# Expert feed-forward with 216 token slots an expert and both token parts under one weight load

## Chip, cores and metric

The kernel runs on one core of one Trainium2 chip. The metric is device time in microseconds (us) of one execution, the median of several runs. Five engines work side by side, each in its own order: PE (TensorE: matmuls, with weight loads listed apart as PEld), DVE (VectorE), ACT (ScalarE), POOL (GpSimd) and SP, which here only issues DMA transfers.

## What is computed

Retention-style linear attention over 2 x 768 tokens with 8 heads, then a top-1 mixture of 8 experts, then a dense feed-forward. The middle part is what the change is about:

```
x: (1536, 512)   cap = 384   E = 8   w1: (8, 512, 1024)   w2: (8, 1024, 512)
expert_idx = argmax(x @ w_gate)              # one expert a token
disp[e, counts[e]] = x[i]                    # first cap tokens of each expert
h = relu(disp @ w1[e]);  y = h @ w2[e]
out[i] = gate_w[i] * y[expert_idx[i], pos[i]]
h2 = out @ w_in;  result = (h2 * sigmoid(h2)) @ w_out   # w_in (512, 2048), w_out (2048, 512), float64
```

With the inputs that are timed, the eight experts get 183, 196, 188, 167, 213, 180, 203 and 206 tokens.

## The kernel before

Float32 operands are split exactly into two `float32r` parts, `hi` (ACT rounds a copy) and `lo` (DVE or POOL subtracts `hi` from the value), and a product is three matmuls: hi by hi, lo by hi, hi by lo. All queues run in the order in which the program is written (`manual_schedule`).

**Attention and routing** come first: scores, values, state, gate, each token's expert and place. A table of tokens by slot (`toki`) then lets POOL gather each expert's rows from DRAM (`gather`, L494). A branch (L674) leads to a general path for tokens beyond the main slots, `over > capm`; it is stepped over when no expert has more than `capm` tokens.

**The expert stage** walks 64 weight units of 128 x 1024 float32, eight an expert: four of `w1` (`stage_a`) and four of `w2` (`stage_b`). SP loads units into five raw buffers; `moe_piece` makes `hi` on ACT (L151) and `lo` (L155) on DVE, on POOL for the first two units alone, into a ring of five. `advance(u)`, at the head of each stage, issues the `hi` of unit u + 3 and the `lo` of unit u + 2. Every sixth stage from the tenth it also issues one piece of the second feed-forward's weights (`ffn_piece`: three operations on ACT, four on DVE, two on POOL, L174 to L190).

The slots are two blocks of 128 an expert, `SL` = 256, held transposed as `xthi` and `xtlo`. `stage_a` (L813 to L817) makes 24 matmuls of 256 columns into one PSUM bank `h`; ACT takes `relu` from the bank into `hhi` (L820), DVE makes `hlo` from the bank and `hhi` (L821). `stage_b` makes 24 matmuls with `three` (L800 to L802) into `y`; `finish` (L842, L843) splits `y` into `x2hi` on ACT and `x2lo` on DVE. After the second `stage_b` of an expert `xprep` transposes the next expert's rows on PE (L774) and `split_x` (L562, L563) splits them. PSUM is eight single banks in rotation.

**The second feed-forward** follows: `s1` and `s2`, three matmuls of 512 columns a product, with ACT and DVE work between (L908 to L911) and the rest of the weight pieces beside it; POOL scatters the rows of the output (L938).

Of the kernel before, what the change touches and what calls it, by code (L numbers as in the profile page):

```python
# [32 lines left out]
# tiles whose tokens get into the first expert's slots by products, not through memory  # L33
# [4 lines left out]
NG = 3  # L38
GT = NTOK // NG

GW = P + E
# float32 numbers around this one are P apart
# [9 lines left out]
def shape_constants(nblk):  # L52
    import numpy as np

    nw = max(E * nblk, NT)
# [26 lines left out]
def moe_chain_kernel(ctx: ExitStack, tc: tile.TileContext, cap: int, a, out: bass.AP):  # L82
# [3 lines left out]
    cap = max(0, min(cap, NTOK))  # L86
    nblk = max(1, -(-cap // P))
    nmain = min(2, nblk)
    capm = min(cap, nmain * P)
    SL = nmain * P  # L90
# [7 lines left out]
    cst = const.tile([P, C_W + max(E * nblk, NT)], F32, name="cst")  # L98
# [5 lines left out]
    blk_base = cst[:, C_W : C_W + E * nblk]  # L104
# [3 lines left out]
    toki = const.tile([P, E * nblk], I32, name="toki")  # L108
# [21 lines left out]
    def load_ffn(u, h):  # L130
        q, r = divmod(u - NMU, 4)
        t = conv[0].tile([P, UNIT], I32, tag="raw64", name=f"raw{u}_{h}", bufs=3 if nblk <= 5 else 2)
# [14 lines left out]
    def moe_piece(u):  # L147
# [4 lines left out]
        lo_eng = nc.gpsimd if u < 2 else nc.vector  # L152
# [6 lines left out]
    def ffn_piece(u, h):  # L159
# [13 lines left out]
        # the low word's part of the significand, and 2 ** exponent (0 below float32's range)  # L173
# [20 lines left out]
    class Feed:  # L194
        """Loads and splits pieces in order; each piece's last part follows the next piece's first."""
# [35 lines left out]
    # ================= attention, gate, routing =================  # L231
# [90 lines left out]
    ohbs = att.tile([P, NT, E * nblk], F16, tag="ohbs", name="ohbs", bufs=1)  # L322
# [73 lines left out]
    def gate(i, fill):  # L396
        """the steps of `fill` run in the gaps of this chain of short operations"""
# [50 lines left out]
    def place(i):  # L448
# [10 lines left out]
        if i >= NT - NPATCH:  # L459
# [6 lines left out]
        # the slot's block, rounded down by adding and subtracting ROUND, as its first slot  # L466
# [4 lines left out]
        # the token's row; dropped tokens have 0: they add nothing to a slot that another may have  # L471
        tok = pm[:, 0:1]
        nc.vector.tensor_scalar(
            out=tok, in0=pf, scalar1=float(cap), scalar2=cst[:, C_TOK + i : C_TOK + i + 1], op0=ALU.is_lt, op1=ALU.mult
# [16 lines left out]
    def gather(pool, e, j, tag, table, n=NT):  # L491
        col = e * nblk + j
# [8 lines left out]
    def first_rows():  # L501
        """the first expert's rows as far as the tiles go that aren't patched"""
# [14 lines left out]
    # expert weights asked for by the last tiles: few, the stores and gathers come first  # L517
# [47 lines left out]
    # the first expert's rows, transposed: one-hot products for the patched tiles, and what was fetched  # L565
# [51 lines left out]
    class Places:  # L617
        """main[p, i]: the place of token i * P + p, if it has a main slot, less its position"""

        def __init__(self, pool, name, keep):  # L620
            self.eo = pool.tile([P, NT, E], F32, name=f"eo_{name}")
            # where only one table is looked up, the mask needn't be kept
# [19 lines left out]
        def per_token(self, dst, table):  # L642
            """dst[p, i] = table[p, expert of token i * P + p]"""
# [25 lines left out]
    # ---- general path: tokens beyond the slots that the main path has, and dropped ones  # L669
# [21 lines left out]
            # places of tokens with position >= capm, and of those that are dropped  # L691
# [377 lines left out]
```

## Time and profile before

| what | value |
|---|---|
| runs | 551.15, 551.33, 552.55 us, median 551.33 |
| span of the profiled execution | 551.5 us, the one core's time from first to last instruction |
| PE busy / weight loads busy | 535.4 us (97%) / 480.1 us (87%) |
| DVE / ACT / POOL busy | 328.3 us (60%) / 249.0 us (45%) / 152.4 us (28%) |
| mean granted TensorE clock | 0.992 |
| HBM read and written | 69.21 MB and 6.29 MB |

The profile is of one execution, and its span is the time that the runs' median gives, to 0.2 us. A row of a group gives how often an operation ran, the busy time of all of them, the mean of one, and the idle time of its engine just ahead of them with what ended it. Back-to-back operations of one engine overlap at their ends in the records, so the pace of a row of operations is read from start to start, not from the mean duration.

### The profile page before, as it was taken

The page shows a single profiled execution, that of the slowest core. Times are in us where ns is not written, and L with a number is a line of the kernel's source. Part 1 is how long each engine was busy: PE and PEld are TensorE (multiplying, and loading weights), DVE is VectorE, ACT ScalarE, POOL GpSimd, SP SyncE. Part 2 cuts the span into 40 slices and gives each one's busy share as a digit, 9 for nine tenths or more (in the row PEclk, how much of TensorE's full clock was granted, in tenths as well). Part 3 has the DMA queues.
Part 4 walks back from the last instruction along what each step waited for, and adds up shares of the span by engine and source line. Part 5 has one row for each costly group of instructions (what it writes and reads, how often), then busy time and mean ns, then how long its engine had stood idle before and what let it go on. Part 6 is the DMA issues. An engine that isn't in the chain of part 4 may idle for free.

```text
span 551.5 us, 9130 instructions
## 1 busy us (share of the span) xinstructions
PE 535.4 (97%) x3510; PEld 480.1 (87%) x3510; DVE 328.3 (60%) x667; ACT 249.0 (45%) x404; POOL 152.4 (28%) x147
## 2 busy tenths in 40 slices
PE   7999986999999999999999999999999999999995
PEld 5899986999999999999988888888888888888885
DVE  3456772678797777777527675546466665342431
ACT  1343542465566566665525655654444543222210
POOL 3343551010441224302102352422313322000215
PEclk9999997999999999999999999999999999999999
DMA  7999963395767766675102231311212200000103
GB/s 214 240 280 302 328 200 125 119 345 191 262 215 245 245 213 235 216 265 168 74 1 76 76 115 50 104 48 68 76 39 76 77 1 0 1 0 1 76 20 134
DMA packets 31889, 76.15 MB, mean 138 GB/s; under 512 B 3745, under 2 KB 12833, under 8 KB 31842
## 3 DMA queue, kind: packets, MB, share of 16 engines
q1 hardware_dynamic: 28944, 67.40, 38.1%
q0 software_dynamic: 2336, 7.60, 4.1%
q8 instruction: 30, 0.49, 0.4%
q10 hardware_dynamic: 562, 0.51, 0.3%
q14 instruction: 17, 0.14, 0.1%
HBM read 69.21 MB, written 6.29 MB: 137 GB/s over the span
## 4 chain that ended last, share of the span: by engine, by line
PE 66%; issue 14%; POOL 2%; DVE 1%; POOLq 0%; ACT 0%; DVEq 0%; ACTq 0%
PE s L800 10%; PE s L802 10%; PE s L801 10%; PE h L813 6%; PE h L814 6%; PE h L817 6%; PE y L800 5%; PE y L801 5%; PE y L802 5%; POOL out L938 1%; PE xp L774 1%; POOL lo L190 0%; POOL w L186 0%; POOLq L1065 0%; DVE gv L909 0%
## 5 line engine op out<-in xcount | busy, mean ns | idle before, releaser
L186 POOL TENSOR_TENSOR w<-w,ex 128x512 f32<-128x512 f32 x32 | 41.4, 1294 | 235.7 <-DVE ex L183 225.6
L909 DVE TENSOR_TENSOR gv<-s,gv 128x512 f32<-128x512 f32 x48 | 33.2, 691 | 90.1 <-ACT gv L908 90.0
L155 DVE TENSOR_TENSOR lo<-raw,hi 128x1024 fp32r<-128x1024 f32 x62 | 80.3, 1310 | 3.1 <-issue 2.4
L800 PE MATMUL s<-x2hi,hi 128*128 128x512 f32 x192 | 75.4, 393 | 0.0
L802 PE MATMUL s<-x2hi,lo 128*128 128x512 f32 x192 | 75.4, 393 | 0.0
L801 PE MATMUL s<-x2lo,hi 128*128 128x512 f32 x192 | 75.3, 392 | 0.0
L908 ACT ACTIVATE gv<-s 128x512 f32<-128x512 f32 x48 | 28.7, 598 | 101.1 <-PE s L802 101.1
L800 PE MATMUL y<-hhi,hi 128*128 128x256 f32 x256 | 72.3, 282 | 0.0
L801 PE MATMUL y<-hlo,hi 128*128 128x256 f32 x256 | 71.6, 280 | 0.0
L802 PE MATMUL y<-hhi,lo 128*128 128x256 f32 x256 | 71.6, 280 | 0.0
L800 PE MATMUL s<-hi,ghi 128*128 128x512 f32 x176 | 69.0, 392 | 0.0
L813 PE MATMUL h<-xthi,hi 128*128 128x256 f32 x256 | 64.7, 289 | 4.5 <-PEq L674 4.5
L801 PE MATMUL s<-lo,ghi 128*128 128x512 f32 x176 | 69.0, 392 | 0.0
L802 PE MATMUL s<-hi,glo 128*128 128x512 f32 x176 | 68.9, 392 | 0.0
L151 ACT CAST hi<-raw 128x1024 fp32r<-128x1024 f32 x64 | 65.5, 1047 | 2.9 <-issue 2.2
L814 PE MATMUL h<-xthi,lo 128*128 128x256 f32 x256 | 64.4, 288 | 0.0
L911 DVE TENSOR_TENSOR glo<-gv,ghi 128x512 fp32r<-128x512 f32 x48 | 36.7, 765 | 33.0 <-ACT ghi L910 28.1
L813 PEld LDWEIGHTS h<-xthi,hi 128*128 128x128 f32 x256 | 50.6, 198 | 4.5 <-issue 4.5
L190 POOL TENSOR_TENSOR lo<-w,hi 128x512 fp32r<-128x512 f32 x32 | 47.6, 1488 | 23.3 <-ACT hi L189 23.3
L814 PEld LDWEIGHTS h<-xthi,lo 128*128 128x128 f32 x256 | 50.5, 197 | 0.0
L801 PEld LDWEIGHTS y<-hlo,hi 128*128 128x128 f32 x256 | 48.6, 190 | 0.0
L800 PEld LDWEIGHTS y<-hhi,hi 128*128 128x128 f32 x256 | 48.6, 190 | 0.0
(140 smaller groups left out, 977.6 us busy)
## 6 DMA issues: line engine op xcount, KB each, us to landing
raw<-w SPq DMA_DIRECT2D x64, 512.0 KB, 4.1
raw<-w_in SPq DMA_DIRECT2D x16, 512.0 KB, 3.5
raw<-w_out SPq DMA_DIRECT2D x16, 512.0 KB, 3.3
vk<-vk SPq DMA_DIRECT2D x11, 512.0 KB, 6.8
xtok<-xr SPq DMA_DIRECT2D x12, 256.0 KB, 5.0
kbd<-kt SPq DMA_DIRECT2D x23, 128.0 KB, 5.7
q<-q SPq DMA_DIRECT2D x11, 256.0 KB, 6.1
gq<-gq SPq DMA_DIRECT2D x10, 128.0 KB, 6.3
```

The source lines that it names most:

```text
L151: nc.scalar.copy(out=hi, in_=t)
L155: lo_eng.tensor_tensor(out=lo, in0=t, in1=hi.bitcast(F32), op=ALU.subtract)
L186: nc.gpsimd.tensor_tensor(out=w, in0=w, in1=ex.bitcast(F32), op=ALU.mult)
L190: nc.gpsimd.tensor_tensor(out=lo[:, sl], in0=w, in1=hi[:, sl].bitcast(F32), op=ALU.subtract)
L800: nc.tensor.matmul(out_ap, lhsT=lh, rhs=rh, start=first, stop=False, skip_group_check=True)
L801: nc.tensor.matmul(out_ap, lhsT=lh, rhs=rl, start=False, stop=False, skip_group_check=True)
L802: nc.tensor.matmul(out_ap, lhsT=ll, rhs=rh, start=False, stop=last, skip_group_check=True)
L813: nc.tensor.matmul(hb[:, f], lhsT=whi[:, d, f], rhs=xhi[:, d], start=f == 0 and d == 0, stop=False, **skip)
L814: nc.tensor.matmul(hb[:, f], lhsT=wlo[:, d, f], rhs=xhi[:, d], start=False, stop=False, **skip)
L817: nc.tensor.matmul(hb[:, f], lhsT=whi[:, d, f], rhs=xlo[:, d], start=False, stop=d == KD - 1, **skip)
L909: nc.vector.tensor_tensor(out=gv, in0=hb, in1=gv, op=ALU.mult)
L911: nc.vector.tensor_tensor(out=glo, in0=gv, in1=ghi.bitcast(F32), op=ALU.subtract)
```

## The change

An expert's main slots go from 256 to 216 (`SLOTS`), still in two blocks, of 128 and 88; `capm` follows, and the general path's overflow blocks get a token table of their own. The two parts of the tokens, and of `h`, lie in one tile, so that a matmul under the weights' `hi` takes both parts, 2 x 216 columns, into two halves of a bank (`two`); a second one under the weights' `lo` takes the `hi` part, 216 columns, into the second half. The halves are added by ACT (copy of one half to SBUF) and DVE (the other half plus that copy) in `add_parts`; the sum `hs` or `ys` is then split from SBUF, one stage later (`after`, `flush`). PSUM is four pairs of banks in this stage. `lo` of every fourth weight unit (u % 4 == 3) is made by POOL, no longer by DVE. The last expert's `finish` stands ahead of the second feed-forward, not behind its first step.

```diff
+SLOTS = 216
+def slots(cap):
+    cap = max(0, min(cap, NTOK))
+    sl = min(SLOTS, max(1, -(-cap // P)) * P)
+    return cap, -(-sl // P), sl, -(-max(0, cap - sl) // P)
...
-        lo_eng = nc.gpsimd if u < 2 else nc.vector
+        lo_eng = nc.gpsimd if u < 2 or u % 4 == 3 else nc.vector
...
     def split_x(e, tvs):
-        hi = moe.tile([P, KD, SL], F32R, tag="xthi", name=f"xthi{e}")
-        lo = moe.tile([P, KD, SL], F32R, tag="xtlo", name=f"xtlo{e}")
-        xts[e] = (hi, lo)
+        both = moe.tile([P, 2, KD, SL], F32R, tag="xt", name=f"xt{e}")
+        xts[e] = both
+        hi, lo = both[:, 0], both[:, 1]
         for j, tv in enumerate(tvs):
-            cs = slice(j * P, (j + 1) * P)
+            cs = slice(j * P, j * P + widths[j])
+            tv = tv[:, :, : widths[j]]
...
-    ps = ctx.enter_context(tc.tile_pool(name="ps", bufs=8, space=PSUM, reuse_waits="tile"))
+    ps = ps_stack.enter_context(tc.tile_pool(name="ps", bufs=4, space=PSUM, reuse_waits="tile"))
+    def pair(name):
+        return ps.tile([P, 2, 512], F32, tag="ps", name=name)
+    def banks2(name):
+        return pair(name).rearrange("p b (k t) -> p b k t", k=2)
...
+    def two(out_ap, w, x, first, last):
+        whi, wlo = w
+        skip = {"skip_group_check": True}
+        nc.tensor.matmul(out_ap[:, :, :SL], lhsT=whi, rhs=x, start=first, stop=False, **skip)
+        nc.tensor.matmul(out_ap[:, 1, :SL], lhsT=wlo, rhs=x[:, 0], start=False, stop=last, **skip)
+    def add_parts(dst, src):
+        nc.scalar.copy(out=dst, in_=src[:, :, 1, :SL])
+        nc.vector.tensor_tensor(out=dst, in0=src[:, :, 0, :SL], in1=dst, op=ALU.add)
     def stage_a(e, fu):
         u = 8 * e + fu
         advance(u)
+        flush()
...
         for f in range(2):
             for d in range(KD):
-                nc.tensor.matmul(hb[:, f], lhsT=whi[:, d, f], rhs=xhi[:, d], start=f == 0 and d == 0, stop=False, **skip)
-                nc.tensor.matmul(hb[:, f], lhsT=wlo[:, d, f], rhs=xhi[:, d], start=False, stop=False, **skip)
-        for f in range(2):
-            for d in range(KD):
-                nc.tensor.matmul(hb[:, f], lhsT=whi[:, d, f], rhs=xlo[:, d], start=False, stop=d == KD - 1, **skip)
...
-        nc.scalar.activation(hhi, hb, AF.Relu)
-        nc.vector.scalar_tensor_tensor(
-            out=hlo, in0=hb, scalar=0.0, in1=hhi.bitcast(F32), op0=ALU.max, op1=ALU.subtract
-        )
+                two(hb[:, f], (whi[:, d, f], wlo[:, d, f]), xt[:, :, d], d == 0, d == KD - 1)
+        hs = moe.tile([P, 2, SL], F32, tag="hs", name=f"hs{e}_{fu}", bufs=3)
+        hh = moe.tile([P, 2, 2, SL], F32R, tag=f"hh{fu}", name=f"hh{e}_{fu}")
+        add_parts(hs, hb)
+        def later():
+            nc.scalar.activation(hh[:, 0], hs, AF.Relu)
+            nc.vector.scalar_tensor_tensor(
+                out=hh[:, 1], in0=hs, scalar=0.0, in1=hh[:, 0].bitcast(F32), op0=ALU.max, op1=ALU.subtract
+            )
+        after.append(later)
...
     def finish(e, yb):
...
+            ys = moe.tile([P, 2, SL], F32, tag="hs", name=f"ys{e}_{b}", bufs=3)
+            add_parts(ys, yb[b])
+            def later(ys=ys, ds2=slice(2 * b, 2 * b + 2)):
+                nc.scalar.copy(out=x2hi[:, ds2, win], in_=ys)
+                nc.vector.tensor_tensor(
+                    out=x2lo[:, ds2, win], in0=ys, in1=x2hi[:, ds2, win].bitcast(F32), op=ALU.subtract
+                )
+            after.append(later)
...
+    finish(E - 1, yb)
+    flush()
+    ps_stack.close()
+    ps = ctx.enter_context(tc.tile_pool(name="ps1", bufs=8, space=PSUM, reuse_waits="tile"))
...
-        if n == 0:
-            finish(E - 1, yb)
```

How the order moves is seen at three places, on the engines that wait or are waited for in the expert stage. In the names the first number is the expert (`h2_1`: expert 2, second unit) or the unit (`lo21`), and the last one a tile's serial number.

PE, the end of one unit of `stage_a` for expert 2, before:

```order
L813 MATMUL h2_1_2886<-xthi2_2750,hi17_2756 128x256
L814 MATMUL h2_1_2886<-xthi2_2750,lo17_2757 128x256
L813 MATMUL h2_1_2886<-xthi2_2750,hi17_2756 128x256
L814 MATMUL h2_1_2886<-xthi2_2750,lo17_2757 128x256
L817 MATMUL h2_1_2886<-xtlo2_2751,hi17_2756 128x256 x8
```

and in the changed kernel:

```order
L866 MATMUL h2_1_3728<-xt2_3609,hi17_3614 128x2x216
L867 MATMUL h2_1_3728<-xt2_3609,lo17_3615 128x216
L866 MATMUL h2_1_3728<-xt2_3609,hi17_3614 128x2x216
L867 MATMUL h2_1_3728<-xt2_3609,lo17_3615 128x216
```

Three matmuls of 256 columns for each block of the weights became one of 432 and one of 216, in turn.

DVE, `stage_a` of expert 2, before (four units' `hlo`, with the `lo` of units 20 to 22 between):

```order
L821 SCALAR_TENSOR_TENSOR hlo2_1_2912<-h2_1_2886,hhi2_1_2911 128x512
L155 TENSOR_TENSOR lo20_2881<-raw20_2760,hi20_2880 128x1024
L821 SCALAR_TENSOR_TENSOR hlo2_2_2947<-h2_2_2921,hhi2_2_2946 128x512
L155 TENSOR_TENSOR lo21_2916<-raw21_2793,hi21_2915 128x1024
L821 SCALAR_TENSOR_TENSOR hlo2_3_2982<-h2_3_2956,hhi2_3_2981 128x512
L155 TENSOR_TENSOR lo22_2951<-raw22_2849,hi22_2950 128x1024
```

and in the changed kernel:

```order
L871 TENSOR_TENSOR hs2_1_3745<-h2_1_3728,hs2_1_3745 128x432
L163 TENSOR_TENSOR lo20_3721<-raw20_3618,hi20_3720 128x1024
L889 SCALAR_TENSOR_TENSOR hh2_1_3746<-hs2_1_3745,hh2_1_3746 128x432
L871 TENSOR_TENSOR hs2_2_3774<-h2_2_3757,hs2_2_3774 128x432
L163 TENSOR_TENSOR lo21_3750<-raw21_3643,hi21_3749 128x1024
L889 SCALAR_TENSOR_TENSOR hh2_2_3775<-hs2_2_3774,hh2_2_3775 128x432
L871 TENSOR_TENSOR hs2_3_3803<-h2_3_3786,hs2_3_3803 128x432
L163 TENSOR_TENSOR lo22_3779<-raw22_3693,hi22_3778 128x1024
```

Each unit has one more operation on DVE, the add from PSUM (L871), and `hh` is now made of two tiles in SBUF; a `lo` stands between a unit's add and its `hh`.

POOL, the gathers and subtractions around experts 2 to 4 in the changed kernel (before, the rows L163 are not on POOL):

```order
L502 DMA xr0_3_0_3681<-xtok_62,toki_67 128x512
L502 DMA xr1_3_1_3685<-xtok_62,toki_67 128x512
L163 TENSOR_TENSOR lo19_3690<-raw19_3582,hi19_3689 128x1024
L163 TENSOR_TENSOR lo23_3810<-raw23_3724,hi23_3809 128x1024
L194 TENSOR_TENSOR w65_0_3844<-w65_0_3844,ex65_0_3842 128x512
L198 TENSOR_TENSOR lo64_3453<-w64_1_3647,hi64_3452 128x512
```

Two subtractions of 1024 columns an expert joined POOL's queue, between the gathers and the pieces of the second feed-forward's weights.

## Rows read from the trace of the kernel before

**Rows 1.** By stretch: PE, PEld, DVE, ACT, POOL busy us (count); clock, DMA share, GB/s.
```profile
89.60:280.70 191.10, 191.10 (x1605) 191.06 (x1606) 137.47 (x180) 106.44 (x145) 40.55 (x28) 0.98 0.61 206
280.70:545.60 264.90, 264.90 (x1166) 216.84 (x1164) 139.70 (x230) 108.19 (x182) 72.39 (x60) 1.00 0.15 52
```

**Rows 2.** One tile, `xp`: count, duration ns min/median/max, first and last start.
```profile
L774 PE MATMUL xp<-eyewg,xr x56: 272/272/273, 109.3 to 252.1; 128*128 128x128 f32 x56
```

**Rows 3.** Timeline of PE in `stage_a`: start us, duration us, instruction.
```profile
121.69 0.28 PE L813 MATMUL h<-xthi,hi 128*128 128x256 f32 x1
...
122.89 0.28 PE L813 MATMUL h<-xthi,hi 128*128 128x256 f32 x1
```

**Rows 4.** Timeline of PE in the second feed-forward.
```profile
419.93 0.40 PE L800 MATMUL s<-x2hi,hi 128*128 128x512 f32 x1
...
421.08 0.39 PE L802 MATMUL s<-x2hi,lo 128*128 128x512 f32 x1
```

**Rows 5.** Groups of weight loads (PEld): weights of 64 and of 128 columns.
```profile
L369 PEld LDWEIGHTS y<-am,vk 128*64 128x64 f32 x192 | 10.2, 136 | 1.5
...
L363 PEld LDWEIGHTS y<-qg,sbd 128*128 128x128 f32 x80 | 9.7, 191 | 1.1 <-POOL qg L342 1.0
```

**Rows 6.** Groups on PE over the span: a float32 matmul, two records of 128 columns each.
```profile
L363 PE MATMUL y<-qg,sbd 128*128 128x128 f32 x80 | 10.7, 277 | 0.8 <-POOL qg L342 0.8
```

**Rows 7.** Timeline of DVE in expert 3.
```profile
177.38 3.88 DVE L155 TENSOR_TENSOR lo<-raw,hi 128x1024 fp32r<-128x1024 f32 x2
181.78 1.29 DVE L563 TENSOR_TENSOR xtlo<-xp,xthi 128x512 fp32r<-128x512 f32 x2 [0.51 <-ACT xthi L562]
182.98 2.35 DVE L155 TENSOR_TENSOR lo<-raw,hi 128x1024 fp32r<-128x1024 f32 x2
```

**Rows 8.** Groups on DVE in the expert stage.
```profile
L155 DVE TENSOR_TENSOR lo<-raw,hi 128x1024 fp32r<-128x1024 f32 x61 | 79.1, 1311 | 2.4 <-issue 2.4
L821 DVE SCALAR_TENSOR_TENSOR hlo<-h,hhi 128x512 fp32r<-128x512 f32 x32 | 22.1, 690 | 29.8 <-ACT hhi L820 29.6
...
L180 DVE SCALAR_TENSOR_TENSOR w<-w,lf 128x512 f32<-128x512 int32 x8 | 5.5, 693 | 0.8
...
L177 DVE TENSOR_SCALAR w<-raw 128x512 int32<-128x512 int32 x8 | 3.4, 422 | 0.0
```

**Rows 9.** Groups on POOL from 60 us to the end of the expert stage.
```profile
L190 POOL TENSOR_TENSOR lo<-w,hi 128x512 fp32r<-128x512 f32 x8 | 16.4, 2055 | 11.8 <-ACT hi L189 11.8
...
L186 POOL TENSOR_TENSOR w<-w,ex 128x512 f32<-128x512 f32 x8 | 10.3, 1294 | 98.5 <-DVE ex L183 98.5
L155 POOL TENSOR_TENSOR lo<-raw,hi 128x1024 fp32r<-128x1024 f32 x2 | 4.7, 2372 | 0.0
```

**Rows 10.** Timeline of POOL at the time of rows 7.
```profile
176.66 1.29 POOL L186 TENSOR_TENSOR w<-w,ex 128x512 f32<-128x512 f32 x1 [11.88 <-DVE ex L183]
177.92 2.27 POOL L190 TENSOR_TENSOR lo<-w,hi 128x512 fp32r<-128x512 f32 x1
```

**Rows 11.** Three lines on DVE: count, duration ns min/median/max, first and last start.
```profile
L155 DVE TENSOR_TENSOR lo<-raw,hi x62: 1209/1216/2309, 87.0 to 272.1; 128x1024 fp32r<-128x1024 f32 x62
...
L911 DVE TENSOR_TENSOR glo<-gv,ghi x48: 691/693/1553, 285.6 to 533.9; 128x512 fp32r<-128x512 f32 x48
...
L909 DVE TENSOR_TENSOR gv<-s,gv x48: 679/692/694, 284.3 to 532.6; 128x512 f32<-128x512 f32 x48
```

**Rows 12.** Groups on ACT in the expert stage.
```profile
L151 ACT CAST hi<-raw 128x1024 fp32r<-128x1024 f32 x60 | 61.3, 1047 | 2.2 <-issue 2.2
L820 ACT ACTIVATE hhi<-h 128x512 fp32r<-128x512 f32 x32 | 19.1, 596 | 42.2 <-PE h L817 42.2
```

**Rows 13.** Waits in the expert stage: who for whom, us in total, times, longest.
```profile
DVE xtlo L563 <- ACT xthi L562: 6.5, 5, 2.9
DVE x2lo L843 <- ACT x2hi L842: 5.2, 3, 1.9
```

**Rows 14.** DMA issues of the page: count, KB each, us to landing.
```profile
raw<-w SPq DMA_DIRECT2D x64, 512.0 KB, 4.1
```

More of the change, by code (lines that the diff above doesn't have):

```diff
@@ L84, in moe_chain_kernel @@
     ctx.enter_context(tc.manual_schedule())
[L86 to L90, printed above, removed]
+    cap, nmain, SL, nover = slots(cap)
+    capm = min(cap, SL)
+    widths = [min(P, SL - j * P) for j in range(nmain)]
     const = ctx.enter_context(tc.tile_pool(name="const", bufs=1))
@@ L489, in place, with gather @@
         )
-    def gather(pool, e, j, tag, table, n=NT):
-        col = e * nblk + j
+    def gather(pool, e, j, tag, table, n=NT, blocks=nmain):
+        col = e * blocks + j
         xr = pool.tile([P, DM], F32, tag=tag, name=f"{tag}_{e}_{j}", bufs=1)
@@ new lines, in moe_chain_kernel @@
+                nc.vector.tensor_tensor(out=slot, in0=slot, in1=block, op=ALU.subtract)
+                nc.vector.tensor_tensor(
+                    out=gohp, in0=iota_p.unsqueeze(1).to_broadcast([P, NT, P]),
+                    in1=slot.unsqueeze(2).to_broadcast([P, NT, P]), op=ALU.is_equal,
+                )
+                gtp = gps.tile([P, 512], F32, tag="gtp", name="gtp", bufs=1)
+                for i in range(NT):
+                    nc.tensor.matmul(
+                        gtp[:, : E * nover], lhsT=gohp[:, i], rhs=gohb[:, i], start=i == 0, stop=i == NT - 1
+                    )
@@ L762, in moe_chain_kernel @@
     conv[0] = ctx.enter_context(tc.tile_pool(name="conv", bufs=1, reuse_waits="tile"))
-    ps = ctx.enter_context(tc.tile_pool(name="ps", bufs=8, space=PSUM, reuse_waits="tile"))
-    def bank(name):
-        return ps.tile([P, 512], F32, tag="ps", name=name)
+    ps_stack = ExitStack()
+    ps = ps_stack.enter_context(tc.tile_pool(name="ps", bufs=4, space=PSUM, reuse_waits="tile"))
[3 more added lines that the diff above has]
+        return pair(name).rearrange("p b (k t) -> p b k t", k=2)
     def xprep(e):
-        tvs = [bank(f"xp{e}_{j}").rearrange("p (d t) -> p d t", d=KD) for j in range(nmain)]
+        xp = pair(f"xp{e}")
+        tvs = [xp[:, j].rearrange("p (d t) -> p d t", d=KD) for j in range(nmain)]
         for j, tv in enumerate(tvs):
@@ L828, in stage_b @@
         advance(u)
+        flush()
         whi, wlo = [t.rearrange("p (f d m) -> p f d m", f=2, d=KD) for t in unit_tiles.pop(u)]
-        hhi, hlo = htiles[fu]
+        hh = htiles[fu]
         for f in range(2):
             for d in range(KD):
-                three(
-                    yb[d // 2][:, d % 2], (whi[:, f, d], wlo[:, f, d]), (hhi[:, f], hlo[:, f]),
-                    fu == 0 and f == 0 and d % 2 == 0, fu == 3 and f == 1,
+                two(
+                    yb[d // 2][:, d % 2], (whi[:, f, d], wlo[:, f, d]), hh[:, :, f],
+                    fu == 0 and f == 0, fu == 3 and f == 1,
                 )
@@ L877, in token_table @@
     def token_table():
-        ct = bank("ct")
+        ct = pair("ct")[:, 0]
         for i in range(NT):
@@ L973, in moe_chain_kernel @@
             token_table()
-        yb = [bank(f"y{e}_{j}").rearrange("p (d t) -> p d t", d=2)[:, :, :SL] for j in range(2)]
+        yb = [banks2(f"y{e}_{j}") for j in range(2)]
         for fu in range(4):
@@ L982, in moe_chain_kernel, with bank @@
             finish(e, yb)
+    finish(E - 1, yb)
+    flush()
+    ps_stack.close()
+    ps = ctx.enter_context(tc.tile_pool(name="ps1", bufs=8, space=PSUM, reuse_waits="tile"))
+    def bank(name):
+        return ps.tile([P, 512], F32, tag="ps", name=name)
     moe_stack.close()
@@ L1017, in layouts @@
     cap = int(inputs["moe_capacity"])
-    nblk = max(1, -(-max(0, min(cap, NTOK)) // P))
     def c(x):
```

72 lines of the change are left out of this document (47 added, 25 removed).

## The prediction

> **What bounds the kernel now.** I read the busy time by stretch first. In the expert stage PE is busy for all of its 191.1 us, at clock 0.98, while DVE has 137 us of work, ACT 106 us and POOL 41 us; in the second feed-forward PE is busy throughout as well [rows 1]. So a matmul saved in the expert stage is time saved, as long as no other engine takes over, and the second feed-forward, which the change leaves alone, stays. Next is the pace of an expert: the transposes, eight an expert, start at 109.3 us and the last of them at 252.1 us; six experts lie between, less the 0.8 us within the last eight, so (252.1 - 0.8 - 109.3) / 6 = 23.7 us each [rows 2]. Of it some 0.9 us are the transposes (eight at hardly more than 0.11 us), and 192 matmuls of 256 columns share 22.8 us, 0.119 us each. The timeline agrees: ten starts in 1.20 us [rows 3].
>
> **PE after the change.** Each of the 64 weight blocks an expert takes one matmul of 432 columns and one of 216 in place of three of 256. A matmul of 512 columns follows the last after 0.230 us (five starts in 1.15 us [rows 4]), one of 256 after 0.120 us, so a column is 0.43 ns and 432 columns are 0.120 + 176 x 0.43 ns = 0.196 us. No `float32r` matmul under 256 columns is in the trace. By columns alone 216 would be 0.103 us. But each has its own weight load: loading 128 columns takes 191 ns where 64 take 136 ns [rows 5], so 64 columns are 55 ns and 128 are 110 ns, and the next load has only this short matmul to hide behind. I take 0.112 us; the bounds are 0.103 us (columns) and 0.120 us (no cheaper than 256). An expert on PE is then 64 x (0.196 + 0.112) + 0.9 = 20.6 us (20.0 to 21.1), 3.1 us less than now. If that were all, eight experts would save 25 us.
>
> **DVE's own work.** Back to back, a second `lo` of 1024 columns adds 2.35 - 1.22 = 1.13 us and a second operation of 512 columns 1.29 - 0.69 = 0.60 us [rows 7, 8, 11]; so 432 columns are 0.52 us. In a middle expert (1 to 6) DVE now has 8 `lo` (9.0 us), 4 `hlo` and 2 `x2lo` (3.6), 2 `xtlo` (1.2) and 8/6 of a piece of the later weights, each two operations like L180 and two like L177, less 0.09 us overlap apiece (1.9 us a piece, 2.5) [rows 8]: 16.3 us. After: 6 `lo` (6.8), 6 adds, 4 `hh` and 2 `x2lo` of 432 columns (6.2), `xtlo` on 216 columns (1.0), the pieces (2.5): 16.5 us. What POOL takes over, the adds give back.
>
> **POOL and DVE stand in each other's way.** This is the term that decides. POOL's work in a middle expert rises from 8/6 x 2 x 1.29 = 3.4 us to 8.2 us, by two `lo` of 2.37 us [rows 9]. While POOL ran two operations, two `lo` on DVE took 3.88 us, not 2.35 us, and POOL's second one took 2.27 us, not 1.29 us [rows 7, 9, 10]: one waits for the other. Over the stage a `lo` goes up to 2.31 us from a median of 1.22 us, and `glo`, also made of two SBUF tiles, from 0.69 to 1.55 us, while L909, which reads PSUM and one SBUF tile, never passes 0.694 us [rows 11]. So `lo`, and by its operands `hh` and `x2lo` after the change (before, they read PSUM), wait for POOL; the adds and `xtlo` don't. DVE lost 1.53 us of POOL's 2.58 us in that spot, 59%; over the whole stage, where DVE often had nothing queued, 61 x (1.311 - 1.216) = 5.8 us of POOL's 16 x 1.29 = 20.6 us, 28% [rows 8, 9, 11]. With DVE busy nearly always I take 59%: 4.8 us of an expert. The bounds are 28% and 100%.
>
> The Trainium skill (SBUF — State Buffer, Who interferes with whom) says more: the port pair that DVE and GpSimd share is an exclusive lock, and the second to issue "fully blocks" when DVE has two SBUF inputs. The rows agree on who blocks. If DVE had only such operations, the rule would make the share 100% and the sum below 565 us in place of 545 us; that is the second rival.
>
> **DVE's waits for others.** Its order is fixed, so it also waits ahead of `xtlo` and `x2lo` for ACT: 11.7 us now over seven experts, 1.7 us each [rows 13]. The new add waits in the same manner for PE's last matmul and ACT's copy, with the next unit's `lo` and `hh` queued behind it; where DVE runs late the copy is done by then, so I add nothing (and up to 0.5 us, one copy, six times an expert if DVE is not late, which is then the case where PE sets the pace).
>
> **Sum.** A middle expert on DVE: 16.5 + 4.8 + 1.7 = 23.0 us, above PE's 20.6 us and 0.65 us below the 23.7 us of now; six of them save 3.9 us. Expert 0 has no pieces (14.0 + 2.8 + 1.7 = 18.5 us) and could save PE's 3.1 us, the last could as much, but each hands on or inherits a late DVE; I take half, 1.5 us each. Together 6.9 us off the profiled execution's 551.5 us, which is also the runs' median to 0.2 us: 544.6, say **545 us**.
>
> Costed at nothing: ACT's extra six copies (8 conversions of 1.05 us, twelve operations under 0.6 us, `xthi`, the pieces' three operations: below 20 us an expert [rows 12]), hidden as long as DVE is the later one. The raw buffer of a unit now comes free when POOL is done, but its next load lands 4.1 us after issue [rows 14] and is wanted two units, some 5 us, on. The four bank pairs: the second unit of an expert needs `y`'s pair, which one copy and one add free, 1.1 us of the 2.5 us that the first unit gives; past that PE waits there too. The last `finish` now stands ahead of the second feed-forward: four short ACT operations, while the first twelve matmuls (2.8 us) run. The smaller token table: nothing.
>
> **The rivals.** *PE keeps the pace.* If POOL's `lo` mostly fall beside adds, and the share stays at 28%, DVE has 16.5 + 2.3 + 1.7 = 20.5 us, just under PE's 20.6 us, and all eight experts save 3.1 us: **527 us** (522 to 531 by the bounds on the 216 columns; to 538 when DVE is the later one here and there). For it: the 28% is what the stage shows now. Against: DVE's slack, 137 of 191 us busy, was what made it so.
>
> *DVE and POOL take longer than PE did.* The same term the other way: above a share of (23.7 - 16.5 - 1.7) / 8.2 = 67% a middle expert is slower than now. At 85% it is 25.2 us, six cost 9 us, the outer two give 3 us back: **557 us**; at 100%, the page's rule, 565 us. For it: POOL doubles its work, six more operations of DVE become ones that wait, and PE then waits for a `lo` in the middle of a unit. Against: a quarter of DVE's time (adds and `xtlo`, 4.2 us) can pass beside POOL.
>
> *The narrow matmul is dear.* A plain float32 matmul of 128 columns, two records, takes 10.7 / 40 = 0.27 us [rows 6]; if a `float32r` one of 216 columns went at that rate it would be 0.45 us, an expert on PE 42 us, and the whole 700 us. Nothing in the rows points to it but that nothing so narrow was run.
>
> *The change doesn't do what it says:* an expert with more than 216 tokens would send all through the general path. The inputs give at most 213.
>
> **How the numbers follow.** 545 us by the forecast with its own range 539 to 550 us (a share of 50 to 70%): 0.48. PE keeps the pace: 0.22. DVE and POOL longer: 0.22. Narrow matmul dear: 0.05. The rest, the general path among it: 0.03. The range 526 to 560 us holds nearly all of the first, some 0.16 of the second, 0.15 of the third: 0.79. A measurement here tells 0.3%, 1.7 us, from no change. Faster by more: 0.41 of the first and all of the second, 0.63. Within: 0.06 of the first, 0.05 of the third and 0.03 elsewhere, 0.14. Slower: 0.23.
>
> **What would show it.** Right: the expert stage some 184 us long; PE with gaps that end on `lo` from DVE or POOL; weight blocks at 0.31 us inside a unit; DVE's `lo` at a mean well over 1.4 us and POOL's at over 2.4 us; `hh` sometimes over 1 us, the adds never. The first rival: PE busy all through and the stage near 167 us. The second: a stage of 195 us and more, DVE with hardly an idle stretch. Wrong altogether: 216 columns at over 0.2 us start to start, or gaps of PE that end on ACT or on a DMA.

## The result, and the profile after

The changed kernel takes **558.74 us** (median of 557.97, 558.38, 559.09 and 560.55) against 551.27 us before: a ratio of 1.0133, 95% interval 1.0112 to 1.0155. It is slower by 7.5 us, where 6 us less was forecast.

First the busy time by stretch of the kernel after, to be held against [rows 1]; the columns are PE, PEld, DVE, ACT and POOL busy, the clock, the DMA share and GB/s.

```profile
0.00:87.50 87.50, 77.54 (x742) 70.61 (x743) 53.31 (x256) 33.07 (x76) 37.47 (x58) 0.99 0.88 255
87.50:283.50 196.00, 175.35 (x1092) 164.66 (x1093) 171.90 (x210) 123.25 (x192) 85.10 (x45) 0.97 0.58 201
283.50:550.60 267.10, 267.09 (x1166) 217.15 (x1164) 139.60 (x232) 110.53 (x185) 72.83 (x60) 1.00 0.15 52
```

The expert stage grew from 191.1 to 196.0 us although PE has a third fewer matmuls in it. PE, busy all through before, is now busy for 175 us. DVE went from 137 to 172 us, POOL from 41 to 85 us. The second feed-forward is longer as well, though the change moves nothing there but the last `finish`: 266.8 us from its first matmul to its last, against 264.9 us before (the rows' ends differ by one matmul). The stretch ahead of the experts is 2.1 us shorter; in the runs below it takes 87.5 to 91.6 us, and the 89.6 us of before lie in that spread. The chain of work that ended last tells the same in one line:

```profile
PE 35%; DVE 22%; issue 19%; POOL 3%; ACT 2%; DMA 2%; DVEq 0%; POOLq 0%; ACTq 0%
```

PE was 66% of the chain before and DVE 1%. What PE waits for in the expert stage of the kernel after, from the view of the waits (us in total, times, longest):

```profile
PE y L867 <- DVE lo L163: 8.7, 9, 2.2
...
PE h L867 <- POOL lo L163: 6.1, 2, 3.5
...
PE h L867 <- DVE lo L163: 3.2, 4, 1.7
...
PE y L867 <- POOL lo L163: 2.2, 2, 1.1
```

These are 20.2 of 20.7 us in which PE is idle in the stage, all on a `lo`, 11.9 us of it on DVE's and 8.3 us on POOL's; before, PE was never idle there. Inside a unit the two products run as priced. From the timeline of PE (start us, duration us) of the kernel after, early in expert 2:

```profile
119.75 0.37 PE L866 MATMUL h<-xt,hi 128*128 128x432 f32 x1
119.95 0.26 PE L867 MATMUL h<-xt,lo 128*128 128x216 f32 x1
...
121.28 0.37 PE L866 MATMUL h<-xt,hi 128*128 128x432 f32 x1
```

Five weight blocks in 1.53 us are 0.306 us each. So what PE saves while it works is there; the waits cost more. Who makes `lo` late shows on DVE and POOL. Lines of the kernel after in the expert stage, by source line, with count, duration in ns min/median/max, first and last start:

```profile
L163 DVE TENSOR_TENSOR lo<-raw,hi x45: 1207/1215/3657, 98.7 to 275.2; 128x1024 fp32r<-128x1024 f32 x45
...
L889 DVE SCALAR_TENSOR_TENSOR hh<-hs,hh x32: 595/601/3404, 94.4 to 278.6; 128x432 fp32r<-128x432 f32 x32
...
L917 DVE TENSOR_TENSOR x2lo<-ys,x2hi x14: 595/598/2811, 115.7 to 267.0; 128x432 f32 x14
...
L871 DVE TENSOR_TENSOR hs<-h,hs x32: 593/596/608, 93.0 to 274.7; 128x432 f32<-128x432 f32 x32
...
L163 POOL TENSOR_TENSOR lo<-raw,hi x16: 2356/2401/3112, 88.7 to 275.2; 128x1024 fp32r<-128x1024 f32 x16
```

The three operations with two SBUF inputs have a usual time and a long tail; the add, with one input in PSUM, has none. Here is one of the long ones in the timelines of the kernel after, DVE, then POOL, then PE (start us, duration us, idle time ahead):

```profile
219.07 0.59 DVE L871 TENSOR_TENSOR hs<-h,hs 128x432 f32<-128x432 f32 x1
220.29 3.40 DVE L889 SCALAR_TENSOR_TENSOR hh<-hs,hh 128x432 fp32r<-128x432 f32 x1 [0.63 <-ACT hh L888]
223.62 0.59 DVE L871 TENSOR_TENSOR hs<-h,hs 128x432 f32<-128x432 f32 x1
```

```profile
219.84 1.00 POOL L502 DMA_INDIRECT xr<-xtok,toki  x1 [0.30 <-issue]
220.86 2.36 POOL L163 TENSOR_TENSOR lo<-raw,hi 128x1024 fp32r<-128x1024 f32 x1
```

```profile
220.28 0.37 PE L866 MATMUL h<-xt,hi 128*128 128x432 f32 x1
223.27 0.55 PE L867 MATMUL h<-xt,lo 128*128 128x216 f32 x1 [2.63 <-POOL lo L163]
```

POOL's `lo` ends at 223.22 us, and only then do both PE's matmul that needs it start and DVE's `hh` get done, 3.40 us for 0.60 us of work. By the records `hh` started 0.57 us ahead of that `lo`, while POOL was at its gather; why it was not done first, no run tells. All 28 operations of DVE in this stage that took over 0.15 us more than the shortest of their kind lay beside a subtraction or product of POOL; they make 41.0 of the 41.8 us that follow.

One number sums this up in every run below. **What DVE loses** is the sum over its operations in the expert stage of their time less the shortest time of the same line and shape; **POOL's own work** is the number of its subtractions and products (not its gathers) by the shortest time of each. An operation that runs once counts as losing nothing: `cohp`, part of the output tokens' masks, takes 1.75 us in the change and in e1, but 3.44 us in e10 and 3.95 us in e9, so these two lose some 2 us more than the table below says. Before, that is 6.9 us lost at 20.7 us of work; after, 41.8 us (18.2 at `lo`, 13.4 at `hh`, 9.7 at `x2lo`) at 58.4 us, 72%.

### The profile page after: what moved, and what is told of

Same layout as the page of the kernel before. It is cut to its first block, busy times and chain, and to the rows that moved or that the text cites. A ratio compares the mean times of both kernels' runs of the same rounds, so it can differ in the third digit from the quotient of the medians.

```text
span 555.9 us, 8225 instructions
## 1 busy us (share of the span) xinstructions
PE 520.0 (94%) x2998; PEld 452.4 (81%) x2998; DVE 365.2 (66%) x699; ACT 266.9 (48%) x452; POOL 196.8 (35%) x163
## 4 chain that ended last, share of the span: by engine, by line
PE 35%; DVE 22%; issue 19%; POOL 3%; ACT 2%; DMA 2%; DVEq 0%; POOLq 0%; ACTq 0%
PE s L851 10%; PE s L852 10%; PE s L853 10%; DVE lo L163 9%; DVE hh L889 3%; DVE hs L871 3%; DVE x2lo L917 2%; POOL out L1014 1%; PE y L866 1%; DMA raw<-w_in 1%; POOL lo L163 1%; PE h L866 1%; DVE ys L871 1%; PE y L867 1%; ACT hh L888 1%
## 5 line engine op out<-in xcount | busy, mean ns | idle before, releaser
L866 PE MATMUL h<-xt,hi 128*128 128x432 f32 x256 | 85.3, 389 | 3.5 <-ACTq L683 3.3
L866 PE MATMUL y<-hh,hi 128*128 128x432 f32 x256 | 81.2, 373 | 0.0
L867 PE MATMUL h<-xt,lo 128*128 128x216 f32 x256 | 70.5, 276 | 9.5 <-POOL lo L163 6.1
L867 PE MATMUL y<-hh,lo 128*128 128x216 f32 x256 | 68.4, 267 | 11.0 <-DVE lo L163 8.7
L163 DVE TENSOR_TENSOR lo<-raw,hi 128x1024 fp32r<-128x1024 f32 x46 | 73.4, 1603 | 2.8 <-issue 2.0
L163 POOL TENSOR_TENSOR lo<-raw,hi 128x1024 fp32r<-128x1024 f32 x18 | 46.3, 2571 | 50.2 <-ACT hi L159 50.1
L867 PEld LDWEIGHTS h<-xt,lo 128*128 128x128 f32 x256 | 51.9, 203 | 11.7 <-POOL lo L163 6.7
L867 PEld LDWEIGHTS y<-hh,lo 128*128 128x128 f32 x256 | 48.8, 191 | 14.3 <-DVE lo L163 11.6
L866 PEld LDWEIGHTS h<-xt,hi 128*128 128x128 f32 x256 | 51.0, 199 | 6.5 <-ACTq L683 3.4
L198 POOL TENSOR_TENSOR lo<-w,hi 128x512 fp32r<-128x512 f32 x32 | 47.8, 1492 | 11.8 <-ACT hi L197 11.7
L866 PEld LDWEIGHTS y<-hh,hi 128*128 128x128 f32 x256 | 48.1, 188 | 2.1
```

Of the source, the lines that this page charges most:

```text
L163: lo_eng.tensor_tensor(out=lo, in0=t, in1=hi.bitcast(F32), op=ALU.subtract)
L198: nc.gpsimd.tensor_tensor(out=lo[:, sl], in0=w, in1=hi[:, sl].bitcast(F32), op=ALU.subtract)
L866: nc.tensor.matmul(out_ap[:, :, :SL], lhsT=whi, rhs=x, start=first, stop=False, **skip)
L867: nc.tensor.matmul(out_ap[:, 1, :SL], lhsT=wlo, rhs=x[:, 0], start=False, stop=last, **skip)
```

## The experiments

**Theory A**: DVE loses most of the time that POOL works, by its operations with two SBUF inputs, and became the later engine by that. **Theory B**: DVE's longer list, or the longer chain from PE's last matmul over copy, add and Relu, is too much by itself. Ratios are to the kernel before on the same chip, where the change has 1.0133.

| run | two products in | later `lo` on POOL | POOL's own work, us | DVE loses, us | stage, us | time, us | ratio, 95% interval |
|---|---|---|---|---|---|---|---|
| before | none, 256 slots | none | 20.7 | 6.9 | 191.1 | 551.27 | 1 |
| the change | w1, w2 | 16 | 58.4 | 41.8 | 196.0 | 558.74 | 1.0133, 1.0112 to 1.0155 |
| e1 | w1, w2 | none | 20.6 | 12.2 | 179.7 | 543.99 | 0.9825, 0.9781 to 0.9870 |
| e2 | w1, w2 | 31 | 93.2 | 62.6 | 211.5 | 575.02 | 1.0390, 1.0348 to 1.0432 |
| e6 | w1, w2 | left out | 20.6 | 11.4 | 174.4 | 537.95 | 0.9738, 0.9702 to 0.9775 |
| e5 | w1, w2 | 16 | 58.1 | 44.7 | 194.2 | 557.18 | 1.0082, 1.0051 to 1.0114 |
| e10 | w1, w2 | 16 | 58.3 | 24.2 | 190.0 | 553.15 | 1.0032, 1.0007 to 1.0057 |
| e3 | none | none | 20.6 | 8.8 | 179.6 | 542.77 | 0.9820, 0.9762 to 0.9877 |
| e9 | none | 16 | 58.4 | 18.4 | 183.9 | 546.85 | 0.9919, 0.9891 to 0.9947 |

### e1 and e2: the later `lo` back on DVE, and more of them on POOL

```diff
-        lo_eng = nc.gpsimd if u < 2 or u % 4 == 3 else nc.vector
+        lo_eng = nc.gpsimd if u < 2 else nc.vector                  # e1
+        lo_eng = nc.gpsimd if u < 2 or u % 2 == 1 else nc.vector    # e2
```

> The sixteen later `lo` that the change gave to POOL are back on DVE, all else as after the change. Theory A (DVE loses some 72% of the time that POOL works): DVE's own work in the expert stage rises from 172 - 42 = 130 us by 16 x 1.21 = 19 us to 149 us, POOL's own falls from 58 to 20 us, of which DVE loses 10 to 15 us; DVE then has 159 to 164 us, less than the 175 us that PE is busy, so the stage takes 176 to 186 us in place of 196 us and the run 539 to 549 us. `lo` on DVE has a mean under 1.4 us. Theory B (DVE is too slow by its own work and the lock is only in company): 19 us more work on the busiest engine, the stage takes 205 to 215 us, the run 568 to 578 us.

> Every second `lo` on POOL (33 in place of 18), all else as after the change. Theory A (DVE loses some 72% of POOL's time): POOL's own work rises by 15 x 2.37 = 36 us to 94 us, DVE's own falls by 18 us to 112 us, and it loses 62 to 68 us; DVE is busy for 174 to 180 us, 2 to 8 us more than now, and PE's waits for POOL's `lo` come on top: the run takes 561 to 575 us. Theory B (DVE's own work binds): 18 us less of it, the stage goes to PE's 175 to 180 us, the run takes 538 to 544 us.

The groups on DVE of e1 and then of e2, each in its expert stage:

```profile
L163 DVE TENSOR_TENSOR lo<-raw,hi 128x1024 fp32r<-128x1024 f32 x61 | 78.0, 1286 | 2.0 <-issue 2.0
L889 DVE SCALAR_TENSOR_TENSOR hh<-hs,hh 128x432 fp32r<-128x432 f32 x32 | 23.5, 735 | 0.1
```

```profile
L889 DVE SCALAR_TENSOR_TENSOR hh<-hs,hh 128x432 fp32r<-128x432 f32 x32 | 53.8, 1681 | 7.8 <-ACT hh L888 6.5 <-issue 1.3
L163 DVE TENSOR_TENSOR lo<-raw,hi 128x1024 fp32r<-128x1024 f32 x30 | 46.4, 1547 | 2.4 <-issue 2.4
```

Sixteen `lo` more on DVE, 19 us more of work, and the stage is 16 us shorter; fifteen fewer, and it is 15.5 us longer. That is theory A's direction in both, and theory B's in neither. `hh` alone went from 23.5 to 53.8 us with its own list unchanged. In e2 the time came out at the very upper end expected: DVE was busy for 179.7 of 211.5 us, and PE waited 8.8 us for POOL's own `lo` besides.

### e6: POOL's `lo` left out

```diff
         def second():
+            if u >= 2 and u % 4 == 3:
+                nc.scalar.copy(out=lo, in_=t)
+                return
```

> The sixteen later `lo` of POOL are left out: in their place ACT copies the raw weights into the low part (so the low part of those weights is wrong). POOL loses 38 us of work, ACT gains 16 x 1.05 = 17 us, DVE's list is that of the change. Theory A (DVE loses time to POOL): DVE falls from 172 us to 140 to 145 us, PE binds with 175 us, the stage takes 175 to 181 us and the run 537 to 544 us. Theory B (DVE is late by its own list or by the chain from PE's last matmul over copy, add and Relu): nothing is gained, 553 to 560 us.

The same view of busy time as above, for e6's expert stage:

```profile
87.80:262.20 174.40, 169.44 (x1092) 162.56 (x1093) 140.30 (x210) 138.18 (x208) 41.27 (x29) 0.98 0.66 226
```

DVE has the change's list to the operation (210 records) and is busy for 140.3 us in place of 171.9. Its list was never too long for PE; only POOL's work is gone, and the time falls by 4% against the change. That is theory A, with ACT taking 15 us more. But the run also takes away PE's waits for POOL's late `lo`, 8.3 us in the change; e10 parts the two.

### e10: the sums written back into PSUM

```diff
-        nc.vector.tensor_tensor(out=dst, in0=src[:, :, 0, :SL], in1=dst, op=ALU.add)
+        nc.vector.tensor_tensor(out=src[:, :, 0, :SL], in0=src[:, :, 0, :SL], in1=dst, op=ALU.add)
+        return src[:, :, 0, :SL]
...
-        add_parts(hs, hb)
+        hs = add_parts(hs, hb)
...
-            add_parts(ys, yb[b])
+            ys = add_parts(ys, yb[b])
```

> The kernel after the change, POOL's eighteen `lo` included, with one edit: DVE's adds write their sum back into the first half of the PSUM bank and not into SBUF, so `hh` and `x2lo` have one operand in PSUM, as `hlo` and `x2lo` had before the change. The number of operations is the same on every engine. Theory A (only DVE operations with two SBUF inputs wait for POOL): `hh` and `x2lo` stay under 0.65 us each, the 23 us that they lost are gone, `lo` loses as much as now or up to 10 us more, DVE is busy for 150 to 160 us in place of 172, the stage takes 180 to 188 us, the run 543 to 551 us. Theory B (DVE loses a share of POOL's time whatever its operands, since its list is full): the same 42 us in other places, 554 to 561 us.

Lines of e10 by source line, as above:

```profile
L163 DVE TENSOR_TENSOR lo<-raw,hi x45: 1207/1216/3940, 97.8 to 269.2; 128x1024 fp32r<-128x1024 f32 x45
...
L890 DVE SCALAR_TENSOR_TENSOR hh<-h,hh x32: 593/598/608, 93.9 to 270.3; 128x432 fp32r<-128x432 f32 x32
...
L918 DVE TENSOR_TENSOR x2lo<-y,x2hi x14: 590/596/602, 116.4 to 260.9; 128x432 f32 x14
```

The same operations, the same POOL work, and `hh` and `x2lo` lose nothing any more; `lo`, still with two SBUF inputs, loses 20.9 us where it lost 18.2. So which operand sits where decides who waits, as the Trainium skill has it (SBUF — State Buffer, Who interferes with whom: a DVE instruction with two SBUF inputs contends with a GpSimd instruction that reads SBUF, one with at most one, outside the two-port modes, does not). DVE's 155 us are as expected; the time is not, by 2 us. PE's waits in e10's expert stage say why:

```profile
PE h L867 <- POOL lo L163: 5.1, 2, 2.6
PE h L866 <- DVE x2lo L918: 3.9, 3, 1.6
...
PE y L866 <- DVE hh L890: 2.5, 1, 2.5
PE y L867 <- DVE lo L163: 2.2, 1, 2.2
```

PE still waits 5.6 us for POOL's `lo`, which the edit does not touch. The banks come free only after `hh` and `x2lo`, and PE now waits 6.4 us for these: a wait that took the place of part of the one removed.

### e3 and e9: the slots alone, without and with POOL's `lo`

e3 is the change with the three products, the eight single banks and the direct `hhi`, `hlo`, `x2hi`, `x2lo` of before, on 216 slots; e9 adds POOL's `lo`.

```diff
-                two(hb[:, f], (whi[:, d, f], wlo[:, d, f]), xt[:, :, d], d == 0, d == KD - 1)
+                nc.tensor.matmul(hb[:, f], lhsT=whi[:, d, f], rhs=xhi[:, d], start=f == 0 and d == 0, stop=False, **skip)
+                nc.tensor.matmul(hb[:, f], lhsT=wlo[:, d, f], rhs=xhi[:, d], start=False, stop=False, **skip)
...
+                nc.tensor.matmul(hb[:, f], lhsT=whi[:, d, f], rhs=xlo[:, d], start=False, stop=d == KD - 1, **skip)
```

> 216 slots with the three products, the copies and the banks of before, and all `lo` after the first two on DVE: the change without its two products. PE has 192 matmuls of 216 columns an expert. Theory A (a matmul of 216 columns costs its columns, 0.098 us, as the trace of the change shows behind one of 432): 19.7 us an expert with the transposes, 4 us less than before, DVE with 17 us of its own below that, so the expert stage takes 158 to 166 us and the run 519 to 528 us. Theory B (the loads of 128 columns set a floor of 0.110 us when every matmul is narrow): 22 us an expert, the stage 178 us, the run 536 to 543 us. Theory C (no cheaper than 256 columns): 549 to 553 us.

> The slots alone, with POOL's sixteen later `lo` kept as in the change. PE has the 112 ns pace of the loads and had no gap with the slots alone (542.8 us); DVE has no adds, and its `hlo` and `x2lo` read PSUM, which POOL never held up. Theory A (POOL's `lo` cost time only where DVE is full, by operations with two SBUF inputs): DVE's own work falls by 19 us and it loses at most 72% of 58 us, 42 us, in all under 165 of 180 us: no time is lost, 541 to 546 us. Theory B (a `lo` of 2.4 us and more on POOL is late for PE by itself): PE gets gaps that end on POOL's `lo`, 548 to 556 us.

The timeline of PE in e3:

```profile
119.80 0.27 PE L858 MATMUL h<-xthi,lo 128*128 128x216 f32 x1
119.91 0.28 PE L857 MATMUL h<-xthi,hi 128*128 128x216 f32 x1
120.02 0.27 PE L858 MATMUL h<-xthi,lo 128*128 128x216 f32 x1
120.13 1.06 PE L861 MATMUL h<-xtlo,hi 128*128 128x216 f32 x8
```

That is theory B's time: 0.112 us from start to start, 179.6 us for the stage without one gap, against 0.099 us for the same matmul behind a wide one in the change. That the weight loads set this pace is theory B's reason; no run tests it by itself. So the narrower slots alone bring 1.8%, and e1, which has the two products as well, brings 1.75%: with `lo` on DVE the two products alone add nothing measurable to the narrower slots. In e1 PE is idle for 6.8 us of the stage, and two stretches of some 3.4 us run at half the clock. e9 lies between its two theories: POOL's sixteen `lo` cost 4.3 us of stage where DVE has 128 of 184 us to do. PE waits 1.9 us for POOL's `lo` and 1.3 us for DVE's, so a `lo` that takes twice as long on POOL does cost something by itself. With the two products in place the same sixteen cost 16.3 us of stage (e1 against the change). The share that DVE loses is thus no constant: the same 58 us of POOL's work take 18 us from a DVE whose `hlo` and `x2lo` read PSUM, 24 us in e10 (both by the table), and 42 us in the change.

### e5: ACT's copies first

```diff
             nc.scalar.copy(out=hi[:, :, cs], in_=tv)
+        for j, tv in enumerate(tvs):
+            cs = slice(j * P, j * P + widths[j])
+            tv = tv[:, :, : widths[j]]
             nc.vector.tensor_tensor(out=lo[:, :, cs], in0=tv, in1=hi[:, :, cs].bitcast(F32), op=ALU.subtract)
```

> The kernel after the change with one edit: of a new expert's transposed tokens ACT copies both blocks before DVE subtracts either, so ACT no longer waits for DVE between them (11.8 us of waiting in the stage). Theory A (DVE is the later one, as POOL takes 72% of its own time out of DVE's): ACT's wait was not what anyone waited for, 555 to 559 us. Theory C (the change put ACT into the chain and that wait is the cost): up to 11.8 us off, 547 to 551 us.

Since both parts of the tokens lie in one tile `xt`, ACT's second copy waited for DVE's first subtraction. The wait is gone and the time is 557.18 us, within theory A's 555 to 559. So ACT's wait was not the main cost: of its 11.8 us at most some 3 us came back (a ratio of 1.0082 against 1.0133, with intervals that just touch). e8 put the same edit on e1:

> Both edits: the sixteen later `lo` back on DVE, and ACT's two copies ahead of DVE's two subtractions. With the first edit alone the stage took 180 us, PE had 8.3 us of gaps over a tenth of them and more, nearly all ended by DVE's `lo`. Theory A: ACT's wait still stands beside a DVE that has 158 of 180 us, 540 to 545 us. Theory C (DVE's gaps behind `xt` come from ACT's late copy): the gaps shrink by half or more, 536 to 540 us.

It gave 540.32 us (0.9758, 0.9700 to 0.9816) against e1's 0.9825; PE is idle for 5.7 us of the stage against 6.8 in e1 (by the gaps in the traces; the expectation has 8.3 us), which is far from theory C's half, and the intervals overlap, so the time decides nothing.

### Towards a version that beats both

e7 keeps the two products for the second weights only, where an expert has two sums and not four; e12 writes those two sums into PSUM; e11 is e8 with all sums in PSUM; e14 is e11 with three narrow products for the first weights of experts 0 to 3. All have `lo` on DVE.

```diff
+        if e < 4:
+            h1 = hb[:, :, 0, :SL]
...
+                    nc.tensor.matmul(h1[:, f], lhsT=wlo[:, d, f], rhs=xt[:, 0, d], start=False, stop=False, **skip)
...
+            htiles[fu] = hh
+            return
```

> 216 slots and all later `lo` on DVE as in the run with the slots alone, with the two products only where the second weights pass (32 of 64 weight blocks an expert), so that DVE has two adds an expert and not six, and `hh` is made from PSUM. PE: 32 x 0.307 + 96 x 0.112 + 0.9 = 21.5 us an expert, against 64 x 3 x 0.112 + 0.9 = 22.4 us with the slots alone. Theory A (with DVE below PE each saved matmul counts): 8 x 0.9 = 7 us less than the slots alone, 534 to 538 us. Theory B (two products cost as much in waits as they save, wherever they stand): 541 to 546 us.

> Three edits to the change: the sixteen later `lo` on DVE, ACT's copies of a new expert's tokens first, the sums in PSUM. With the first two DVE still lost 12 us (5.8 at `lo`, 5.6 at `hh` and `x2lo`) and PE had 7 us of gaps. Theory A: DVE loses 6 to 8 us and PE's gaps fall to 3 to 5 us: the run takes 535 to 540 us, ratio to before 0.97 to 0.98. Theory B (the gaps come from the order of DVE's list, with a unit's sum ahead of the next `lo`, and not from POOL): no gain, ratio 0.975 to 0.982; if the later release of the banks makes PE wait, above that.

> The two products only where the second weights pass, with all later `lo` on DVE, and the two sums an expert in PSUM. Without the last edit PE had one gap of 1.0 us in the stage and DVE lost 10.8 us with 142 of 175 us busy. Theory A (PE bound): nothing or up to 1 us to be had, ratio to before 0.97 to 0.977. Theory B (the banks of `y` come free later and PE waits for them): a ratio over 0.98.

> The three edits of the run with `lo` on DVE and the sums in PSUM, and one more: the first weights of experts 0 to 3, beside which DVE also makes the masks of the output's tokens, take three matmuls of 216 columns and no sum; those of experts 4 to 7 and all second weights keep the two products. Theory A (a saved matmul counts wherever DVE keeps up): experts 4 to 7 take 20.6 us each as in that run, the others 21.5 to 22.9 us as in the run with two products in the second weights only, the stage 170 to 172 us, ratio to before 0.965 to 0.972. Theory B (DVE or the banks set the pace in the early experts in any case): a ratio of 0.973 to 0.978.

| run | stage, us | time, us | ratio, 95% interval |
|---|---|---|---|
| e7 | 175.0 | 539.21 | 0.9747, 0.9685 to 0.9809 |
| e11 | 174.7 | 538.42 | 0.9756, 0.9732 to 0.9780 |
| e12 | 174.3 | 537.00 | 0.9731, 0.9705 to 0.9757 |
| e14 | 172.2 | 535.73 | 0.9693, 0.9658 to 0.9729 |

All four stages are shorter than e3's 179.6 us; in their times e12 and e14 are clear of e3, while the intervals of e7 and e11 overlap its own. e7 falls between its two theories: the stage is 4.6 us shorter, not 7. e11's ratio fits both of its theories; DVE loses 6.0 us, as theory A has it, but PE stays idle for 5.8 us, 2.6 us of them at one `hh` that freed a bank late. e12 and e14 fit their theories A. In e14 PE is busy for all but half a microsecond of the stage (the row leaves out its first 0.3 us):

```profile
91.40:263.30 171.90, 171.49 (x1221) 167.23 (x1220) 145.76 (x210) 114.04 (x175) 40.14 (x28) 0.98 0.69 229
```

Experts 4 and 5 start at 181.49 and 202.09 us and expert 6 at 222.69 us, 20.60 us apart. At 3.1% under the kernel before it has the lowest ratio measured, though its interval still overlaps those of e7, e8 and e12.

## Why the prediction was wrong

**PE after the change: right.** 0.308 us a weight block was forecast and 0.306 us measured, 20.6 us an expert against 20.60 us in e14, where nothing holds PE up. The split was another: start to start 0.208 us behind a matmul of 432 columns (0.196 forecast) and 0.099 us behind one of 216 (0.112). The prediction's 0.112 us, which it took from the load of the weights, shows where narrow follow narrow, in e3; behind a wide matmul it does not.

**DVE's own work: too small by 1.2 us an expert, the first step that failed.** For the six middle experts of the kernel after, 113.27 to 261.82 us, the row of busy time is

```profile
113.27:261.82 148.55, 131.55 (x830) 123.01 (x829) 140.16 (x166) 99.19 (x156) 70.04 (x37) 0.98 0.64 224
```

that is 24.76 us an expert, of which DVE is busy 23.36 us. It loses 34.0 us there, 5.67 an expert, so its own work is 17.7 us and not "16.5 us". Some 0.9 us of the difference is work that the sum left out, the output tokens' masks and the offsets, 5.5 us in all, the longest of which are, in the groups on DVE of that stretch,

```profile
L940 DVE TENSOR_TENSOR cohp<-cst,csplit 128x1536 f16<-128x1536 f32 x1 | 1.7, 1746 | 0.0
L945 DVE TENSOR_TENSOR cohb<-cst,csplit 128x144 f16<-128x144 f32 x1 | 1.4, 1396 | 0.0
```

They cost nothing before, when DVE had slack, and count once it is the later engine. (L945 takes 0.30 us in e1 and e10, so 1.1 us of the 5.5 is one more wait for POOL.) The sum could have been held against the trace before, where the six middle experts' row is

```profile
109.30:251.30 142.00, 142.00 (x1214) 141.96 (x1213) 112.35 (x143) 86.22 (x119) 38.95 (x27) 1.00 0.71 238
```

DVE's 112.35 us, less the 6.7 us lost there, are 17.6 us an expert, where the prediction's sum has 16.3 us. That the adds give back what POOL takes over was right: 17.6 us and 17.7 us.

**"With DVE busy nearly always I take 59%: 4.8 us of an expert": the second.** In the middle experts DVE lost 5.67 us, 71% of POOL's 47.7 us, and the whole stage gives 72%. The 59% came from one spot of the trace before [rows 7, 10], where only `lo` had two SBUF inputs. The change makes six more operations an expert into such ones. The prediction named them, but carried the share over as if they were not there; e10 measures that case, 24.2 of 58.3 us, 41%.

The three terms: 17.7 + 5.7 + 1.4 us idle (1.7 forecast) give 24.8 us where 23.0 us was forecast; of the 1.8 us, 1.2 are own work and 0.9 the share, less 0.3 of waits. Six such experts are 10.6 of the 13.7 us between forecast and measurement. Either term alone would have brought an expert to 24.2 or 23.9 us, no faster than the 23.7 us of before. The prediction had put the break-even at a share of 67% and the case above it as its second rival (557 us at 85%); that rival's stage, 195 us and more with DVE hardly idle, is what came, at a smaller share and with the forgotten work on top. The cause is still POOL's `lo`: e1 gives DVE 16 us more work of its own and e6 none, and both are faster than before. That it holds up DVE is one part, as e10 shows; that PE waits for the slower `lo` itself is the other (8.3 us in the change, 5.6 us in e10).

**The outer experts: less than taken.** Expert 0 took 25.8 us and expert 7 21.7 us; 1.5 us each was forecast against before, and 0.6 and 1.0 came.

**Costed at nothing: right, but for what the terms above hold.** No PE wait on the second raw buffer, on the bank pairs of the change, or on ACT beyond the stage's start is in the waits. The second feed-forward's 1.9 us stay unexplained: the same 1164 matmuls, without a gap, start 229.4 ns apart in the mean in place of 227.8. Every run with 216 slots has 266.8 us there against 264.9 us in the one profile of before, with the slots alone too, so neither the place of the last `finish` (e3 has it where it was) nor the two products make it.

**The base: right by luck.** A run takes some 2 us more than its span (557.97 against 555.9 us), so the profiled execution before, with a span of 551.5 us, stands for a run of some 553.5 us; that its span is the runs' median of 551.3 us is chance. The two profiles therefore lie 4.4 us apart and the medians 7.5 us; of these the expert stage's 4.9 us and the second feed-forward's 1.9 us are seen in the traces.

**The rivals.** PE did not keep the pace, a narrow matmul is not dear (0.099 to 0.112 us), and the tokens fit the slots. The second rival is told above.

## What to carry to other kernels

Before an operation goes to POOL, list which DVE operations have two SBUF inputs after the change: each of them can wait for a whole POOL operation, and a result that is moved from PSUM to SBUF makes its readers such operations. A share of lost time read where DVE has slack or a different mix does not hold when it is full; take break-even as the question and ask which way each added operation pushes. And try the parts apart: here the narrower slots alone gave 1.8%, and the two products added to it clearly only in e12 and e14, with `lo` on DVE and fewer sums, written into PSUM.

## What was not expected of the hardware

The granted clock fell to half twice in the middle of the expert stage, behind PE's two longest gaps (3.5 us ended at 148.28 us, 2.6 us at 223.27 us). Stretches of the kernel after:

```profile
147.90:151.30 3.40, 3.02 (x10) 2.88 (x11) 3.40 (x5) 1.92 (x3) 0.32 (x1) 0.50 0.52 163
...
223.00:226.40 3.40, 3.13 (x11) 2.98 (x12) 3.40 (x6) 1.92 (x3) 0.22 (x1) 0.50 0.51 160
```

That is 1.2 of 2.4 GHz. Between 148.62 and 150.92 us the timeline has four weight blocks, 0.575 us each in place of 0.306. From 148.28 to 151.31 us PE got ten matmuls done, which are 1.5 us at the full clock, so each stretch costs 1.5 us more after the wait itself has ended. The length of the last gap does not decide it alone: in e1 the clock was 0.50 from 126.05 to 129.40 us behind a gap of 1.7 us, while in e11 it stayed at 1.00 from 174.40 us on behind one of 2.6 us. e2, with 26.1 us of waits, has a mean clock of 0.93 in the stage.

An operation with one SBUF input was held up too, though seldom. L183 in e10, of eight operations (same columns as above):

```profile
L183 DVE TENSOR_SCALAR ex<-raw x8: 414/420/2102, 118.7 to 247.4; 128x512 int32<-128x512 int32 x8
```

The one of 2.10 us, at 227.5 us, lay beside a `lo` on POOL for 1.82 us; another took 1.08 us, and e2 and e9 have one of 2.62 us each. So the adds and the operations that read PSUM are the ones that pass freely here, not every operation with a single SBUF input. The Trainium skill (SBUF — State Buffer, Who interferes with whom) names `tensor_scalar` among the operations that can contend, when their operands meet certain conditions; this row agrees.

A weight block of a wide and a narrow matmul is cheaper than the narrow one's price among its like suggests: 0.099 us behind 216 columns in the change, 0.112 us in e3. That the load of the narrow one's successor hides behind the wide matmul would explain it; no run tested that.
